# A reduction over three numbers for the softmax sums, and another order of work, in a fused attention, expert and gated-convolution kernel

## The chip, the cores and the metric

One core of a Trainium2 chip runs one program. The metric is the device time of one execution in microseconds (us), as the median of several runs. Five engines work side by side: TensorE (PE, matmuls), VectorE (DVE), ScalarE (ACT), GpSimd (POOL), and SyncE (SP), which here only issues DMAs.

## What is computed

Three layers on a batch of 4 with 576 positions, in float32. Cut to what matters:

```
# 1. attention, 8 heads of 64, twice per head: on q, k, v averaged by 4, and in a band of |i-j| < 4
out_up    = repeat(softmax(q_d @ k_d.T / 8) @ v_d, 4)
out_local = softmax(where(band, q @ k.T / 8, -1e9)) @ v
x = (out_up + out_local) laid out as (4, 576, 512)
# 2. four experts with causal attention, each position takes its best two
for e in range(4):
    s = where(causal, -1e9, (x @ wq[e]) @ (x @ wk[e]).T / 8);  s -= s.max(-1)
    a = exp(s);  a /= a.sum(-1) + 1e-09
    out += gate(e) * (a @ (x @ wv[e]) @ wo[e])
# 3. gated convolution with 5 taps
gate = 1 / (1 + exp(-conv(out)))
y = (gate * (out @ w_val)) @ w_out
```

## The kernel before

Nearly every product is done in three matmuls: both operands are split into a high and a low part in a faster 32-bit type, and high x high, low x high and high x low are summed in PSUM (`mm3`, its matmuls at L1228, L1229 and L1230). The split is a cast (L798) and a subtraction (L815), on an engine of choice. The weights w_val, w_o and w_out come in a 64-bit type; `chunk` (L817) loads their raw words and makes float32 of them: two absolute values on ACT (L854, L859), two steps on DVE (L863, L867), an addition on POOL (L871) and a merge on DVE (L875). `weights_tail` (L889) multiplies w_o by w_val (L896) once, so that layer 2 ends in w_o x w_val. `weights_qkv` loads and splits the experts' weights wqk and wvg.

The attention goes through four batches and four pairs of heads. For each pair the q and k rows are averaged (L946, L953, giving qd and kd), the averaged scores are made on PE (L1083), their maximum is taken on DVE (L1007) and scaled by the scale factor (L1017, on ACT or POOL), the exponentials are made on ACT, either with the sum (L1022) or without (L1028, the sum then on DVE at L1042 or L1044), normalized (L1070 or on ACT at L1068), transposed on PE (L1099) and copied out of PSUM (L1106, pdT). L1117 multiplies by v. The band's part does the same in blocks of 64 rows: scores at L1142 and L1148, transposes at L1161, copies at L1168 (pT), values at L1183; L1200 adds the two parts into a row, which is then split into xh and xl for the experts.

The experts go over two pairs of experts (pr) and five tiles T of 128 queries (the last has 64). `expert_scores` makes the scores (L1380), `exponentials` masks them and finds the extremes (L1410) and makes the exponentials with their sums on ACT (L1419). `weigh` (L1468) adds EPS to the sums, takes the reciprocal (L1491) and multiplies the exponentials by it and the gate's weight (L1520, or on ACT at L1517). For the last tile, two experts lie one under the other on the partitions and the sum comes in two pieces, one per half of the keys, in a buffer of the pool `es`. `keys_on_rows` transposes the weighted exponentials (L1441, into two PSUM banks) and copies them out (the helper `copy`, L790, buffer mp), and L1552 multiplies them by the values (vE). The gated convolution follows: taps at L1600 to L1619, the product with w_out, and a copy (L1646) and store (L1652) of the result.

The order of all this isn't the order of the code. Each step is a `piece` with an engine, a cost in us, and the buffers it reads and writes. `Plan.order` (L358) goes through a model of the five engines; where an engine is free it takes, of the pieces whose inputs and buffers are there, the one with the earliest entry in the table `DUE` (L34), one entry for each of 2773 pieces in the order of their creation. Where a step can go to several engines, `pick` (L311) takes the option whose number stands in the string `PICK` (L255), 1008 characters. The instructions are then issued in the order found, and each engine works through its own in that order. The numbers of the buffers and PSUM banks (ps_63 to ps_70) follow from it.

```
p = Piece(engine, cost, late, (DUE[idx] if idx < len(DUE) else 0.0, idx), fn, k, size)
...
k = min(int(PICK[n]), len(options) - 1) if n < len(PICK) else 0
```

Of the kernel before, what the change touches and what calls it, by code (L numbers as in the profile page):

```python
# [21 lines left out]
EPS = 1e-9  # L22
# [12 lines left out]
    0.3, 1.5, 0.7, 5.45, 1.6, 0, 0.15, 3.85, 3.6, 5.2, 4.58, 0.5, 6.19, 2, 3.88, 4.83, 0, 1, 9.28, 4.5,  # L35
    16.58, 3.52, 4.1, 6.05, 6.81, 0.5, 1.5, 6, 22.88, 5, 4.59, 5.08, 6.73, 7.22, 17.54, 18.54, 7.78,
    10.77, 11.82, 12.71, 12.29, 12.29, 14.5, 15.06, 15.35, 10.26, 11.2, 11.67, 11.89, 12.93, 14.04,
    14.63, 14.92, 16.62, 18.95, 18.53, 21.15, 22.48, 24.1, 12.93, 15.14, 15.84, 16.3, 16.3, 15.74,
    15.74, 16.3, 18.4, 19.77, 19.98, 15.54, 16.14, 16.14, 16.14, 16.3, 18.17, 19.37, 20.11, 20.98,
    21.27, 22.24, 23.25, 23.67, 24.3, 25.31, 25.72, 29.93, 30.84, 26.62, 27.82, 28.67, 29.8, 19.93,  # L40
    21.38, 22.41, 22.86, 22.88, 21.98, 21.98, 22.88, 24.96, 26.51, 26.86, 21.77, 22.37, 24.74, 22.81,
    22.37, 22.37, 22.81, 26.84, 27.4, 27.62, 28.69, 30.31, 30.41, 31.47, 32.48, 32.71, 33.81, 34.55,
    32.6, 35.41, 36.28, 37.2, 14.58, 16.08, 25.52, 29.42, 29.92, 19, 19.57, 22.52, 23.1, 21.38, 21.88,
    26.02, 33.48, 32.48, 26.15, 28.09, 27.07, 28.76, 38.08, 39.1, 25.08, 26.61, 27.49, 28.05, 27.82,
    27.2, 27.2, 27.82, 30.15, 32.11, 32.82, 27, 29.09, 30.66, 29.47, 27.6, 27.6, 29.47, 33.14, 33.4,
    33.62, 30.15, 31.59, 32.53, 33, 32.99, 34.03, 35.12, 36.22, 36.51, 32.2, 33.65, 34.31, 34.31, 35.7,
    36.42, 37.11, 37.42, 39.01, 40.64, 40.64, 43.37, 45.19, 45.36, 41.49, 42.74, 43.77, 44.96, 46.38,
    46.38, 47.01, 47.83, 46.38, 46.81, 47.39, 47.9, 34.03, 36.31, 37.91, 38.37, 38.41, 36.91, 36.91,
    39.9, 40.54, 41.15, 41.44, 36.71, 38.34, 38.81, 42.74, 37.31, 37.31, 44.12, 44.72, 45.59, 45.88,
    47.39, 48.66, 49.08, 49.87, 50.88, 51.19, 52.95, 53.68, 50.88, 50.88, 51.49, 51.88, 8.78, 16.41,  # L50
    16.83, 2.5, 7.96, 8.58, 4, 14.11, 14.72, 2, 7.58, 8.04, 23.38, 32.18, 34.17, 3, 8.93, 9.66, 22.38,
    29.18, 30, 15.08, 19.59, 20.38, 0, 6.42, 6.65, 6.88, 6.19, 5.5, 3.5, 10.65, 11.27, 11.42, 11.89,
    12.43, 13.81, 14.7, 18.02, 17.08, 15.58, 21.3, 21.85, 22.17, 22.9, 23.64, 25.02, 27.4, 25.97, 35.97,
    26.52, 39.99, 39.44, 41.24, 41.71, 42.79, 44.52, 50.65, 48.22, 62.46, 68.35, 72.56, 73.44, 73.47,
    74.01, 74.55, 75.98, 76.87, 79.31, 78.06, 0, 79.68, 80.5, 0, 81.49, 25.02, 31.29, 36.67, 28.92,
    38.23, 39.56, 91.07, 95.14, 95.28, 95.87, 96.51, 97.05, 98.35, 98.89, 98.73, 103.73, 104.59, 104.68,
    105.49, 106.54, 108.62, 110.24, 111.36, 45.41, 54.53, 55.08, 55.3, 56.23, 56.77, 58.25, 59.13,
    59.78, 59.13, 63.3, 63.85, 64.07, 64.78, 65.52, 67.02, 70.22, 70.96, 76.87, 81.7, 82.25, 82.63,
    84.21, 85.88, 87.59, 90.08, 91.52, 65.82, 66.18, 66.54, 66.9, 68.83, 68.15, 61.71, 62.07, 63.23,
    65.46, 66.35, 67.23, 57.48, 57.84, 58.2, 58.56, 60.29, 61.81, 53.46, 53.82, 54.54, 55.79, 56.81,  # L60
    60.56, 31.01, 38.28, 49.42, 54.18, 56.96, 54.82, 69.17, 69.57, 68.61, 69.91, 71.18, 71.73, 69.39,
    69.77, 72.45, 73.28, 73.82, 74.35, 74.87, 75.46, 80.78, 86.85, 69.38, 72.38, 72.73, 73.09, 73.99,
    74.54, 67.77, 68.23, 68.58, 69.73, 70.76, 70.32, 71.4, 73.44, 73.8, 74.15, 74.51, 75.65, 77.73,
    62.43, 63.59, 63.95, 65, 65.69, 65.69, 66.69, 35.55, 40.41, 52.92, 55.34, 59.18, 59.75, 58.94,
    59.51, 56.57, 57.15, 68.94, 70.09, 70.53, 71.83, 73.12, 72.61, 75.06, 54.9, 56.15, 56.59, 57.03,
    59.74, 62.55, 60.61, 62.88, 60.01, 62.31, 60.28, 60.83, 61.27, 62.79, 64.72, 64.4, 66.76, 7.44,
    7.33, 75.07, 76.67, 77.37, 76.94, 77.71, 78.06, 78.66, 78.55, 79.15, 79.82, 80.28, 80.55, 81.28,
    80.55, 81.83, 80.55, 81.43, 80.55, 82.35, 84.81, 86.38, 86.94, 89.84, 91.58, 92.29, 94.55, 95.43,
    99.19, 81.02, 82.36, 82.87, 82.09, 83.22, 83.81, 86.47, 85.07, 87.06, 87.75, 88.6, 88.88, 89.98,
    89.28, 90.6, 88.88, 90.96, 88.88, 89.22, 92.83, 94, 93.62, 94.92, 96.19, 96.19, 96.85, 97.13, 98,  # L70
    87.32, 88.67, 91, 89.38, 91.73, 94.37, 95, 95.27, 96.2, 95.27, 97.18, 98.5, 99.23, 99.31, 91.95,
    93.13, 94.48, 93.87, 95.52, 97.22, 99.77, 100.05, 103.44, 100.05, 101.53, 106.64, 109.82, 107.8,
    93.33, 96.78, 95.07, 98.53, 99.11, 99.6, 101.15, 104.61, 105.42, 105.83, 106.13, 107.27, 108.59,
    110.76, 113.29, 117.58, 117.19, 118.22, 111.81, 114.29, 116.07, 113.17, 116.63, 117.9, 119.75,
    120.02, 120.76, 120.02, 120.12, 125.38, 127.44, 126.58, 116.85, 117.91, 119.34, 118.65, 120, 121.41,
    121.93, 122.23, 124.79, 122.13, 124.17, 128.2, 129.16, 128.95, 118.11, 122.42, 119.38, 123.13,
    123.62, 126.11, 126.96, 127.71, 128.18, 128.46, 128.46, 129.82, 130.39, 131.42, 133.4, 135.96,
    135.96, 136.76, 32.98, 33.98, 40.59, 54.73, 61.46, 42.03, 43.17, 45.21, 45.72, 34.97, 35.47, 40.09,
    60.96, 61.96, 46.71, 47.61, 49.91, 50.48, 51.61, 52.74, 46.15, 48.26, 48.85, 49.2, 49.2, 48.85,
    48.85, 49.2, 51.29, 52.61, 53.33, 49.51, 50.11, 51.07, 50.56, 50.11, 50.11, 50.56, 53.19, 54.92,  # L80
    58.55, 51.61, 54.04, 54.69, 57.22, 55.02, 55.02, 60.22, 61.1, 62.84, 53.53, 54.56, 55.63, 54.89,
    54.89, 61.19, 61.72, 62.28, 64.3, 65.23, 65.84, 75.86, 77.3, 77.51, 67.26, 69.88, 70.2, 77.83,
    78.83, 78.95, 80.31, 82.86, 78.83, 79.38, 79.93, 80.8, 58.92, 60.08, 60.68, 60.68, 60.68, 61.32,
    61.92, 63.12, 65.04, 65.75, 66.04, 61.91, 63.2, 68, 63.67, 62.51, 62.51, 63.67, 70.62, 71.09, 72.2,
    80.27, 81.01, 81.35, 81.92, 82.93, 83.38, 84.3, 85, 82.93, 83.08, 83.92, 87.12, 48.12, 47.62, 54.23,
    78.83, 79.33, 57.39, 60.48, 55.04, 56.01, 59.96, 60.46, 53.73, 82.93, 90.57, 64.41, 64.98, 68.25,
    68.81, 61.02, 77, 70.97, 72.77, 75.58, 76.04, 76.05, 76.05, 77.97, 78.46, 79.24, 72.25, 73.03,
    74.25, 73.37, 73.37, 75.85, 77.2, 78.17, 83.58, 84.55, 85.47, 86.19, 88.31, 91.56, 78.61, 80.75,
    82.8, 83.27, 83.56, 81.35, 81.35, 85.98, 86.92, 87.41, 87.7, 80.35, 81.15, 84.59, 81.48, 80.95,
    80.95, 81.48, 86.99, 87.5, 88.89, 91.08, 92.56, 92.71, 93.95, 95.15, 95.44, 96.46, 97.23, 95.15,  # L90
    96.2, 96.84, 98.35, 88.42, 90.56, 91.16, 91.16, 91.16, 91.91, 92.9, 94.6, 96.85, 97.51, 97.8, 91.18,
    91.78, 91.78, 91.78, 92.31, 93.26, 97.6, 99.11, 99.84, 100.7, 102.31, 103.05, 103.39, 104.34,
    105.35, 105.93, 106.8, 107.4, 105.45, 105.91, 107.78, 110.42, 97.26, 99.82, 100.44, 100.41, 101.05,
    100.41, 101.84, 100.41, 102.63, 100.41, 103.82, 105.14, 103.63, 103.98, 106.69, 107.49, 108.42,
# [1618 lines left out]
```

## Time and profile before

| | |
|---|---|
| median of 3 runs | 355.61 us (353.96 to 356.92) |
| profiled execution | 357.07 us, its span 355.4 us |
| PE busy | 332.9 us (94%) |
| DVE busy | 297.4 us (84%) |
| ACT busy | 257.8 us (73%) |
| POOL busy | 204.7 us (58%) |
| mean granted TensorE clock | 0.974 |

The span runs from the first to the last recorded instruction; 1.7 us of the execution lie around it. Busy times are shares of the whole span, so a view by windows is needed to see in which stage an engine is short of work. In the rows, L12 is line 12 of the kernel before; "A <- B" behind an idle time names the instruction whose end let A start. The granted clock is 1.00 at 2.4 GHz and 0.50 at 1.2 GHz.

### The profile page before, as it was taken

The numbers are of one execution on the slowest core, as the hardware profiler recorded it, in microseconds if no ns is written. First come the engines' busy times: TensorE is split into PE (matmuls) and PEld (weight loads), VectorE is DVE, ScalarE is ACT, GpSimd is POOL, SyncE is SP. The second block draws the span as 40 slices with busy tenths as digits, with TensorE's granted clock in tenths as the row PEclk, the third lists the DMA queues.
The fourth block names the chain that finished last, engine by engine and source line by source line (L and its number), as shares of the span: only waits on it lengthen the run. The fifth ranks groups of instructions, "written<-read, shape, count | busy, mean of one in ns | idle before, by whom it ended". The sixth has DMA issues, their size and how long they took to land.

```text
span 355.4 us, 11539 instructions
## 1 busy us (share of the span) xinstructions
PE 332.9 (94%) x4360; PEld 290.8 (82%) x4360; DVE 297.4 (84%) x921; ACT 257.8 (73%) x923; POOL 204.7 (58%) x325
## 2 busy tenths in 40 slices
PE   0697899998999999999999999999999999999996
PEld 0464679876698898999898897998998899997896
DVE  6898998899999899988989786898887668799572
ACT  3778968689888987688786797466765565688462
POOL 7357867559879852477978432384673036444070
PEclk9999589997899999999999999999999999999999
DMA  7979948519431344236222110101000100001022
GB/s 264 258 217 236 235 137 184 155 61 195 110 85 50 91 123 113 52 107 169 65 91 68 50 51 2 39 4 70 9 0 5 44 0 17 0 4 57 15 65 74
DMA packets 26279, 31.70 MB, mean 89 GB/s; under 512 B 2672, under 2 KB 18032, under 8 KB 26224
## 3 DMA queue, kind: packets, MB, share of 16 engines
q1 hardware_dynamic: 26224, 30.97, 32.4%
q8 instruction: 34, 0.56, 0.7%
q14 instruction: 21, 0.17, 0.2%
HBM read 26.24 MB, written 4.72 MB: 87 GB/s over the span
## 4 chain that ended last, share of the span: by engine, by line
PE 81%; DVE 9%; POOL 4%; ACT 3%; issue 2%; POOLq 0%; DVEq 0%
PE ps L1228 19%; PE ps L1229 17%; PE ps L1230 17%; PE ps L1552 7%; PE ps L1380 5%; PE ps L1441 3%; PE ps L1183 2%; PE ps L1148 2%; PE ps L896 2%; PE ps L1117 1%; PE ps L1161 1%; PE ps L1083 1%; DVE mx L1007 1%; ACT p L1022 1%; PE ps L1099 1%
## 5 line engine op out<-in xcount | busy, mean ns | idle before, releaser
L1419 ACT ACTIVATE pe<-ps,mmin 128x128 f32<-128x128 f32 (+4 forms) x80 | 41.9, 527 | 15.3 <-DVE mmin L1410 10.0
L1612 POOL TENSOR_TENSOR row<-row,row 128x256 f32<-128x256 f32 (+1 forms) x40 | 32.0, 804 | 33.0 <-ACT row L1607 18.4
L1614 DVE SCALAR_TENSOR_TENSOR row<-ps,cw,row 128x320 f32<-128x320 f32 (+1 forms) x88 | 43.3, 513 | 6.2 <-ACT row L1600 4.3
L1228 PE MATMUL ps<-gh,wout_h 128*128 128x256 f32 (+1 forms) x128 | 39.3, 307 | 0.5 <-DVE pT L1168 0.5
L1230 PE MATMUL ps<-xh,wqk_l 128*128 128x256 f32 (+1 forms) x128 | 37.8, 295 | 2.1 <-POOL wqk_l L815 2.1
L1228 PE MATMUL ps<-xh,wqk_h 128*128 128x256 f32 (+1 forms) x128 | 39.1, 306 | 0.6 <-DVE vE L790 0.3
L1229 PE MATMUL ps<-gl,wout_h 128*128 128x256 f32 (+1 forms) x128 | 37.8, 295 | 0.0
L1229 PE MATMUL ps<-xl,wqk_h 128*128 128x256 f32 (+1 forms) x128 | 37.8, 295 | 0.0
L1230 PE MATMUL ps<-gh,wout_l 128*128 128x256 f32 (+1 forms) x128 | 37.7, 294 | 0.0
L1552 PE MATMUL ps<-mp,vE 128*64 128x320 f32 (+4 forms) x224 | 27.0, 374 | 0.0
L1230 PEld LDWEIGHTS ps<-xh,wqk_l 128*128 128x128 f32 x128 | 24.2, 189 | 2.3 <-POOL wqk_l L815 2.3
L1228 PEld LDWEIGHTS ps<-gh,wout_h 128*128 128x128 f32 x128 | 24.1, 188 | 2.5 <-POOL gl L815 0.8
L1228 PEld LDWEIGHTS ps<-xh,wqk_h 128*128 128x128 f32 x128 | 24.1, 189 | 2.2 <-DVE vE L790 0.6
L1520 POOL TENSOR_SCALAR pe<-pe,rs,gw 128x128 f32<-128x128 f32 (+3 forms) x31 | 21.0, 683 | 7.8 <-DVE mmin L1415 4.9
L1007 DVE TENSOR_REDUCE mx<-ps 128x5 f32<-128x320 f32 (+1 forms) x48 | 23.7, 519 | 1.1 <-PE ps L1148 0.6
L1229 PEld LDWEIGHTS ps<-gl,wout_h 128*128 128x128 f32 x128 | 24.1, 188 | 0.2 <-POOL gl L815 0.2
L1229 PEld LDWEIGHTS ps<-xl,wqk_h 128*128 128x128 f32 x128 | 24.2, 189 | 0.0
L1230 PEld LDWEIGHTS ps<-gh,wout_l 128*128 128x128 f32 x128 | 24.1, 188 | 0.0
L1228 PE MATMUL ps<-wvg_h,xh 128*128 128x260 f32 (+1 forms) x80 | 23.5, 293 | 0.6 <-POOL xh L798 0.6
L1552 PEld LDWEIGHTS ps<-mp,vE 128*64 128x64 f32 (+1 forms) x224 | 14.2, 138 | 11.9 <-issue 3.9
L1230 PE MATMUL ps<-wvg_h,xl 128*128 128x260 f32 (+1 forms) x80 | 22.7, 284 | 1.0 <-DVE xl L815 1.0
L1229 PE MATMUL ps<-wvg_l,xh 128*128 128x260 f32 (+1 forms) x80 | 22.6, 282 | 0.0
(231 smaller groups left out, 1208.8 us busy)
## 6 DMA issues: line engine op xcount, KB each, us to landing
qt<-in_qT_dram SPq DMA_DIRECT2D x16, 288.0 KB, 3.7
kt<-in_kT_dram SPq DMA_DIRECT2D x16, 288.0 KB, 4.4
v<-in_vx_dram SPq DMA_DIRECT2D x16, 288.0 KB, 5.3
vw<-in_vx_dram SPq DMA_DIRECT2D x16, 192.0 KB, 4.1
out_dram<-o SPq DMA_DIRECT2D x16, 160.0 KB, 1.8
raw<-in_w_val_dram SPq DMA_DIRECT2D x4, 512.0 KB, 5.1
vw<-in_vx_dram SPq DMA_DIRECT2D x16, 128.0 KB, 3.9
raw<-in_w_out_dram SPq DMA_DIRECT2D x4, 512.0 KB, 3.5
```

Source lines behind the costliest of these rows:

```text
L896: nc.tensor.matmul(pw[m].t, t.t[:, m * P:(m + 1) * P], f.t, start=(c == 0), stop=(c == KC - 1))
L1007: nc.vector.tensor_reduce(out=mx.t[:n, :g, 1], in_=sv(), op=ALU.max, axis=AX.X)
L1228: nc.tensor.matmul(p, ah, bh, start=first, stop=False)
L1229: nc.tensor.matmul(p, ah, bl, start=False, stop=False)
L1230: nc.tensor.matmul(p, al, bh, start=False, stop=last)
L1380: nc.tensor.matmul(s.t[:, o:o + P * (t + 1)], a.t[r, P * t:P * t + P], z.t[r, :P * (t + 1)], start=(k == 0 and t == T[0]), stop=(k == 2 an ...
L1419: nc.scalar.activation(pe.t[:, off + c0:off + c1], s.t[:, o:o + c1 - c0], AF.Exp, bias=m.t[:, 0:1], scale=-1.0, accum_out=sums.t[:, a:a + ...
L1441: nc.tensor.transpose(pt.t[:, i:i + 64], pe.t[r, j * P:(j + 1) * P], ident[r, r])
L1520: ENG[en].tensor_scalar(v, v, x, y, op0=ALU.mult, op1=ALU.mult)
L1552: nc.tensor.matmul(av.t[64 * e:64 * e + 64, z:n], vE.t[:kr, j, 2 * pr + e, :], pT.t[:kr, e, k0:k0 + n - z], start=(j == 0), stop=(j == Tl))
L1612: nc.gpsimd.tensor_add(g.t[:, :nn], g.t[:, :nn], g2.t[:, :nn])
L1614: nc.vector.scalar_tensor_tensor(g.t[:, :nn], x2.t[:, k:k + nn], cw.t[:, m, k:k + 1], g.t[:, :nn], op0=ALU.mult, op1=ALU.add)
```

## The change

Four edits are in the code, and both tables are new. The buffers of `es` get four columns; the third of them holds EPS from the start on, and for the last tile of a pair the two pieces of the sum and EPS are added by one reduction over three columns into the fourth, of which the reciprocal is taken. This happens eight times, once for each batch and pair. Of the 2773 due times 2754 are other numbers, and 443 of the 1008 choices of an engine (or of the order of two things) are others.

```diff
 DUE = (
-    0.3, 1.5, 0.7, 5.45, 1.6, 0, 0.15, 3.85, 3.6, 5.2, 4.58, 0.5, 6.19, 2, 3.88, 4.83, 0, 1, 9.28, 4.5,
+    0.3, 1.8, 0.7, 5.35, 0, 0.5, 0.65, 1.6, 5.95, 6.65, 1.85, 0.8, 6.19, 0, 1.9, 4.15, 0, 1, 6.5, 4.5,
...
 PICK = (
-    "011100000001230000010112021100012002032101000120010100100011231130040010001000000150042211001021"
+    "010100000032210001001202021100012012030100000100000100000031231142040001010101100152040201021021"
...
-        "es": slots("es", 2, [P, 2]),
+        "es": slots("es", 2, [P, 4]),
...
             nc.vector.memset(t[:, :, 1], EPS)
+        for t in pools["es"]:
+            nc.vector.memset(t[:, 2:3], EPS)
...
-                nc.vector.tensor_scalar(sums.t[:, 0:1], sums.t[:, 0:1], sums.t[:, 1:2], EPS, op0=ALU.add, op1=ALU.add)
+                nc.vector.tensor_reduce(out=sums.t[:, 3:4], in_=sums.t[:, 0:3], op=ALU.add, axis=AX.X)
...
-            nc.vector.reciprocal(a, a)
+            nc.vector.reciprocal(a, sums.t[:, 3:4] if last else a)
```

Lines of the changed kernel lie 1 to 3 below those of the kernel before: L857 is L854, L862 is L859, L1020 is L1017, L1444 is L1441. Over the whole program DVE has 905 instructions in place of 923, ACT 775 in place of 747, POOL 333 in place of 330; PE's matmuls and SP's 137 DMAs stay as many.

First place: ACT in the first 15 us, around the first piece of w_val (raw_80 holds its words, o_164 and o_165 the two operands; mx_84 and mx_85 are the maxima of the first averaged scores). Before:

```order
L1527 ACTIVATE ah_157<-ident 128x2x4
L854 ACTIVATE o_164<-raw_80 128x512
L1017 ACTIVATE mx_84<-mx_84 128x3
L859 ACTIVATE o_165<-raw_80,two 128x512
L1017 ACTIVATE mx_85<-mx_85 128x3
L1028 ACTIVATE pd_95<-ps_64,mx_84 128x3x48 x3
L1022 ACTIVATE pd_95,sm_88<-ps_63,mx_85 128x3x48 x3
```

Now:

```order
L1530 ACTIVATE ah_157<-ident 128x2x4
L801 CAST wvg_h<-o_164 128x260
L1020 ACTIVATE mx_84<-mx_84 128x3
L857 ACTIVATE o_164<-raw_80 128x512
L862 ACTIVATE o_165<-raw_80,two 128x512
L1025 ACTIVATE pd_95,sm_88<-ps_64,mx_85 128x3x48 x3
L1031 ACTIVATE pd_95<-ps_63,mx_84 128x3x48 x3
```

The scaling of mx_84 stands ahead of both absolute values (L857, L862), where it stood between them (L854, L859); a split of wvg stands ahead of all, and the scaling of mx_85 is now a reduction on DVE (L1018, L1015 before).

Second place: POOL around the last piece of wqk (o_164 is its load, o_166 is w_o's, p_93 a block of band exponentials). Before:

```order
L815 TENSOR_TENSOR wqk_l<-o_165,wqk_h 128x512
L798 CAST wo_h<-o_166 128x512
L798 CAST wqk_h<-o_164 128x512
L1070 TENSOR_TENSOR p_93<-p_93,sm_90 128x320
L1017 TENSOR_SCALAR mx_85<-mx_85 128x3
L815 TENSOR_TENSOR wqk_l<-o_164,wqk_h 128x512
L1200 TENSOR_TENSOR row_103<-row_103,od_101 128x228
```

Now:

```order
L801 CAST wqk_h<-o_164 128x512
L818 TENSOR_TENSOR wqk_l<-o_163,wqk_h 128x512
L801 CAST wo_h<-o_166 128x512
L1020 TENSOR_SCALAR mx_84<-mx_84 128x3
L1020 TENSOR_SCALAR mx_85<-mx_85 128x3
L1073 TENSOR_TENSOR p_93<-p_93,sm_90 128x320
L818 TENSOR_TENSOR wqk_l<-o_164,wqk_h 128x512
L1203 TENSOR_TENSOR row_106<-row_106,od_101 128x228
```

The cast of the last piece (wqk_h from o_164) has moved ahead of the wait for w_o; its lo part (wqk_l from o_164) still stands behind the cast of w_o, two scalings and the normalization p_93.

Third place: ACT around the second pair's first exponentials of the experts, some 80 us into the run (pe_135 and pe_136 are the exponentials, L1419 or L1422; p_92 and p_93 are blocks of the band's). Before:

```order
L854 ACTIVATE o_164<-raw_80 128x512
L859 ACTIVATE o_165<-raw_80,two 128x512
L1017 ACTIVATE mx_85<-mx_85 128x5
L1419 ACTIVATE pe_135,rs_145<-ps_66,mmin_137 128x128
L1419 ACTIVATE pe_136,rs_145<-ps_67,mmin_141 128x128
L1028 ACTIVATE p_92<-ps_69,mx_85 128x64 x5
L1022 ACTIVATE p_93,sm_89<-ps_65,mx_84 128x64 x5
```

Now:

```order
L862 ACTIVATE o_163<-raw_80,two 128x512
L1020 ACTIVATE mx_85<-mx_85 128x5
L857 ACTIVATE o_164<-raw_80 128x512
L1031 ACTIVATE p_92<-ps_70,mx_85 128x64 x5
L1025 ACTIVATE p_93,sm_88<-ps_63,mx_84 128x64 x5
L1109 COPY pdT_96<-ps_69 112x432
L1422 ACTIVATE pe_135,rs_145<-ps_64,mmin_141 128x128
L1422 ACTIVATE pe_136,rs_145<-ps_65,mmin_137 128x128
L801 CAST wout_h<-o_163 128x512
```

The band's exponentials (L1031, L1025) stand ahead of the experts' (L1422), and a copy of pdT has come to ACT.

On PE, at the same place, the transposes L1441 came right behind the 18 transposes L1099; in the changed kernel the values L1186 (40 small matmuls, L1183 before) stand between them, and the band's scores (L1145 and L1151) stand ahead of L1120 (L1117 before).

## Rows read from the trace of the kernel before

**Rows 1.** The page, parts 1 and 2: busy time by engine; busy tenths of PE by slice.

```profile
PE 332.9 (94%) x4360; PEld 290.8 (82%) x4360; DVE 297.4 (84%) x921; ACT 257.8 (73%) x923; POOL 204.7 (58%) x325
...
PE   0697899998999999999999999999999999999996
...
PEclk9999589997899999999999999999999999999999
```

**Rows 2.** Three windows: us, then busy us (instructions) of PE, PEld, DVE, ACT, POOL; clock; DMA.

```profile
0.00:100.00 100.00, 81.22 (x1270) 63.24 (x1271) 89.33 (x272) 77.05 (x320) 70.80 (x119) 0.91 0.72 184
100.00:350.00 250.00, 249.47 (x3079) 225.66 (x3079) 207.59 (x650) 179.42 (x601) 133.94 (x207) 1.00 0.18 50
350.00:355.40 5.40, 2.19 (x15) 1.93 (x14) 0.49 (x1) 1.31 (x3) 0.00 (x0) 0.90 0.34 121
```

**Rows 3.** PE's waits: line waited for, us in total, times, longest.

```profile
PE ps L1083 <- POOL kd L953: 8.1, 1, 8.1
PE ps L896 <- DVE o L875: 3.2, 1, 3.2
PE ps L1230 <- POOL wqk_l L815: 2.1, 1, 2.1
PE ps L1230 <- DVE xl L815: 1.0, 1, 1.0
PE ps L1441 <- ACT p L1028: 0.7, 1, 0.7
...
PE ps L1441 <- DVE p L1033: 0.7, 1, 0.7
```

**Rows 4.** Windows around the stalls and the low clock, columns as in rows 2.

```profile
34.00:38.00 4.00, 0.88 (x3) 0.38 (x3) 2.92 (x8) 3.13 (x12) 3.93 (x6) 0.86 1.16 230
36.00:48.00 12.00, 10.32 (x159) 8.14 (x159) 11.40 (x23) 8.80 (x32) 9.52 (x12) 0.57 0.85 217
50.00:100.00 50.00, 47.65 (x685) 39.37 (x685) 46.05 (x155) 42.68 (x176) 38.28 (x52) 0.93 0.54 132
84.00:92.00 8.00, 7.27 (x107) 5.48 (x107) 7.55 (x24) 7.95 (x37) 7.67 (x11) 0.57 0.71 126
```

**Rows 5.** PE's timeline: start, us, form, count; in brackets idle before and releaser.

```profile
14.47 2.08 PE L896 MATMUL ps<-o,row 128*128 128x512 f32 x2 [3.20 <-DVE o L875]
...
25.77 1.98 PE L896 MATMUL ps<-o,row 128*128 128x512 f32 x4
```

**Rows 6.** DVE's groups by form: count, busy us, mean ns, idle before and releaser.

```profile
L790 DVE COPY mp<-ps 128x384 f32<-128x384 f32 x15 | 8.0, 551 | 2.1 <-PE ps L1441 2.1
...
L1168 DVE COPY pT<-ps 128x348 f32<-128x348 f32 x15 | 7.4, 508 | 0.3 <-PE ps L1161 0.3
...
L1106 DVE COPY pdT<-ps 112x432 f32<-112x432 f32 x10 | 5.9, 596 | 0.0
...
L790 DVE COPY vE<-ps 128x256 f32<-128x256 f32 x9 | 3.8, 417 | 0.1
...
L1477 DVE TENSOR_SCALAR es<-es 128x1 f32<-128x1 f32 x8 | 1.7, 209 | 1.4 <-ACT pe L1419 1.4
...
L1053 DVE TENSOR_REDUCE sm<-sm 128x5 f32<-128x10 f32 x7 | 1.1, 155 | 0.0
```

**Rows 7.** Timelines of ACT and POOL at the first piece of w_val.

```profile
10.02 0.68 ACT L854 ACTIVATE o<-raw 128x512 f32<-128x512 f32 x1 [1.91 <-DMA raw<-in_w_val_dram]
11.00 0.21 ACT L1017 ACTIVATE mx<-mx 128x3 f32<-128x3 f32 x1 [0.30 <-DVE mx L1007]
...
12.43 1.26 POOL L871 TENSOR_TENSOR o<-o,o 128x512 int32<-128x512 int32 x1 [3.99 <-DVE o L867]
```

**Rows 8.** POOL's timeline around the last piece of wqk.

```profile
31.69 0.61 POOL L798 CAST wo_h<-o 128x512 fp32r<-128x512 f32 x1 [1.40 <-DMA o<-in_wo_dram]
...
34.23 1.26 POOL L815 TENSOR_TENSOR wqk_l<-o,wqk_h 128x512 fp32r<-128x512 f32 x1
```

**Rows 9.** PE's timeline at 82 us.

```profile
81.81 0.91 PE L1183 MATMUL ps<-pT,vw 64*64 64x58 f32 x40
```

More of the change, by code (lines that the diff above doesn't have):

```diff
@@ L34 @@
 DUE = (
[217 rows of a table removed]
[218 rows of a table added]
 )
 PICK = (
-    "011100000001230000010112021100012002032101000120010100100011231130040010001000000150042211001021"
-    "212000102110110000002121012101010100110000111000010000010000001111000000000100111111120211000001"
-    "001011102000101100222011001010001001003203201021101111010210012000120002102100100101110222121110"
-    "400100010010012202220000012000000100000110110110000000100000000001000011200000010000100011111000"
-    "100111001110010100101010010010101012110112122001002000101101201012011112010001011110110111322002"
-    "100132251111101121202220000010010111111010421420222020000000001121212221000110011001210001210111"
-    "110000200000010020000021000021000021101000101100010001110000110010010110011011001001210101111021"
-    "101011220000110011111211012211001010100101010120222130210011011100110140052211001011110100111152"
-    "130201102011010000012132101101011110001021110010101100010010001111110100002101110001000000110110"
-    "110100011101010010111011000010100000011022112010011100010022101001002110002000120100010000001110"
-    "110010002110010011010000210000211111200100000010"
+    "010100000032210001001202021100012012030100000100000100000031231142040001010101100152040201021021"
+    "010111002110112000002101210110010000010111010001001100000010001010000011000100111111110011000001"
+    "000210001000021100212101011010111101000010014200220100000210212204120002102100000001112000021000"
+    "420010000010012202120000002100102100000000100100110100100000010001000001211100200000101110100010"
+    "011000001100110101110010111101102111100002021000002111101200100012000110000010100111111111022322"
+    "010141150201101120202322001010111101000111202400020221000100001110210221111010210000201000201100"
+    "011000210010001001010001000020010000010111110100100010111010101010110110100000010111200110110022"
+    "201000201102001000110211112010020000100011101000240130042001001001100030041210000001111111101142"
+    "240042141101100012010141050110111120100120000111010021011101010101102001112011000100002000011001"
+    "000110111001111111100011111100100000110022002110111001001010100110101001102201110100011000110010"
+    "000000000100102101100100210010211100010100000110"
 )
```

433 rows, old and new, of the table DUE are left out of this document.

## Prediction

> **What bounds the kernel now.** I read the page first: PE is busy for 332.9 of 355.4 us, DVE for 297.4, and in the 40 slices of the span PE falls short of nine tenths mainly in the first quarter and in the last slice [rows 1]. The chain of waits that ended last runs through PE for most of its length, so the views that matter are those that say where PE stands idle and where its clock is low. Three long windows give the first [rows 2]: in the first 100 us PE is busy for 81.22, so idle for 18.8; from 100 to 350 us it is idle for 0.53 of 250; behind 350 us it is idle for 3.2 while the last output is copied and written. An order of work can only win what stands in those 22.5 us, and what a low clock costs. The products are the same: both orders hold equally many matmuls of each form.
>
> PE's waits name the idle time [rows 3]. Its first matmul comes at 8.07 us, when POOL has made the first down-sampled k. It waits 3.2 us for the first piece of w_val made from its 64-bit words, 2.1 and 1.0 us for two lo parts between 34 and 38 us, and 0.7 us twice at L1441. These last two belong to the 2.35 us that PE is idle between 50 and 100 us [rows 4].
>
> The windows from 36 to 48 and from 84 to 92 us have a mean granted clock of 0.57 [rows 4]: the full level (2.4 GHz) gives way to the half (1.2 GHz) and comes back. Taken as all work, 12 x 0.43 = 5.2 us and 8 x 0.43 = 3.4 us of full clock are missing. Ahead of the first fall PE had been busy for 0.88 of 4 us (34 to 38); the second came at about the first wait at L1441, of 0.7 us. At the start the clock row shows nine tenths or more [rows 1], but I go by the durations: a pair of L896 took 2.08 us at 14.47 and four took 1.98 at 25.77 [rows 5], so the first 20 us went at half pace too.
>
> **The four edits of code.** Eight times the sum of two accumulators and a constant goes from a tensor_scalar with its second operand as a scalar per partition (209 ns each) to a tensor_reduce over three numbers of one tile. The nearest row is the reduction of ten numbers to five at L1053, 155 ns [rows 6]. So 8 x 0.05 = 0.4 us leaves DVE; two memsets of one column each come in at the start. All eight places lie behind 100 us, where PE is idle for 0.53 us in all and DVE has 42 us to spare [rows 2]. I take 0; bounds -0.4 and +0.1 (the memsets, if they hold up the first add).
>
> **The order and the engines.** DVE issues 18 instructions fewer, ACT 28 more, POOL 3 more. The largest moves: 12 copies of L790 (8 mp, 4 vE), 5 of L1168 and 3 of L1106 go from DVE to ACT, at 0.55, 0.42, 0.51 and 0.60 us [rows 6]: 4.4 + 1.7 + 2.5 + 1.8 = 10.4 us. Against it casts of qh and normalizations come to DVE, so that some 6 of its 297 us go. In the body that buys nothing, since PE waits for nobody there; what counts is the first 100 us, place by place.
>
> *Start, 0 to 20 us.* POOL's add of the k rows goes to DVE and the loads alternate q and k, so the first of two kd tiles is ready earlier; but PE's first group needs the second kd too, and that stands behind one more add on DVE. No gain taken. For w_val, ACT's scaling of mx now stands ahead of the absolute value that starts the conversion. In the trace the absolute value starts at 10.02 and the scaling only at 11.00, when DVE's maximum is there [rows 7]. So the conversion starts 1.0 us later. Its other operand and POOL's step at 12.43 [rows 7] were waiting for DVE and ACT in any case, so I count half as left: the product starts near 14.95 in place of 14.47. Both its halves then run back to back, where 18 transposes stood between them, and PE has 0.5 us less behind it at 20 us; but it then waits for ACT again, so the loss is mostly covered. I take 0; bounds -0.7 (kd's early half) and +0.8.
>
> *28 to 40 us.* The stall of 2.1 us is the lo part of the last piece of wqk. On POOL it stood behind a wait of 1.40 us for wo from DMA, two casts, a normalization and a scaling, and started at 34.23 for 1.26 us [rows 8]. In the new order the cast of that piece is moved ahead, but the lo part of another piece, the cast of wo with its DMA, two scalings and the same normalization still stand before it. On SP's queue that piece is still the last load of wqk, behind the same bytes. By the same durations it ends between 35.1 and 35.8. I take 0; bounds -1.5 (the wait for wo gone) and +0.5.
>
> *80 to 95 us.* Before, L1441 came right behind the transposes L1099, and PE waited 0.7 us for ACT, which had two w_val steps and two exponentials of L1419 ahead of the one that freed the bank. Now the 0.91 us of L1183 [rows 9] stand between L1099 and L1441 and cover that wait, and ACT has the band's exponentials ahead of those of L1419 (the two w_val steps stay ahead). The second wait has L1441 pulled ahead of the next scores, which may cover it or lay it bare. Of the 2.35 us I take about half as gone, 1.1 us, for this and the lighter DVE together; bounds -2.35 (all) and +1.0 (L1441 bare).
>
> *Body and tail.* 0.1 us of the stall of about 0.5 in the body; bounds -0.5 and +1.5, the upper end being two new stalls of L1441's kind. Between the last w_o product and the first group of the last chunk equally many matmuls stand in both orders, and behind the last matmul come the same copy and stores: 0, within 0.3.
>
> **Sum.** 0 + 0 + 0 - 1.1 - 0.1 = -1.2 us. The profiled execution took 357.07 us (its span of 355.4 and 1.7 around it), so it would take 355.9. It lies 1.46 above the median of the runs, 355.61; the forecast for the median is 354.4. All bounds on one side give -5.8 and +4.2, without the clock.
>
> **Rivals.**
> *A fall of the clock does not come.* Each fall follows thin work. L1183 behind L1099 and the band's scores ahead of L1117 fill the stretch before the second; an earlier lo part of wqk would fill the one before the first. Against it: the stalls at 34 to 38 us stay by my count. Without the second fall 354.4 - 3.4 = 351.0 us; without the first 349.2; without both 345.8.
>
> *The start holds the clock down (the slower side).* Place: the wait for the w_val product, now some 3.7 us long. Price: if the full level comes later by as much work as the fall at 36 us held, 5.2 us, 354.4 + 5.2 = 359.6 us. It decides once the four L896 at 25 us take 4 us in place of 1.98. For it: the pace doubled only after that wait, and the first fall followed a stretch with as little work. Against it: DVE holds the pace until 30 us, so part of the price is hidden, and both halves of the product back to back are denser work than before.
> The Trainium skill (TensorE: Matmul & The Clock Gate, section "HAM oscillation — how this bites in real kernels") says that an engine left waiting between bursts of matmuls is put back to the low clock and runs the start of the next burst at it. The trace agrees at 36 us (0.57). At 14.47 us it cannot tell, since the pace was low already. By the page alone this rival would be the likelier one.
>
> *Nothing takes effect.* The stalls move and add up to the same, and the gain in DVE lies in covered work: 355.6 us.
>
> **How the numbers follow.** One per cent, 3.6 us, is about what a measurement of this kernel tells from no change: faster means under 352.05, slower over 359.2. The forecast, with its own range of 352 to 357, gets 0.48; nothing takes effect 0.15; one fall gone 0.20 and both 0.04; the start holds the clock down 0.13. Nearly all of the falls gone is faster, 0.24, and the forecast's own tail adds 0.06. Of the slow start half stays under 359.2 because part hides behind DVE, so 0.07, and new stalls and the forecast's other tail add 0.06. So faster 0.30, same 0.57, slower 0.13. The range leaves out both falls gone and the end of the slow cases: 348.5 to 358.8.
>
> **What would show it.** Right: PE idle in the first 100 us between 16.5 and 19; the w_val product's first matmul near 14.95; a wait of about 2 us at the lo part of wqk; both dips of the clock still there; at most 0.4 us of wait at the first L1441; 0.6 us or less idle from 100 to 350 us; the new reductions at 140 to 160 ns. Wrong: a wait at L1441 of 1 us; four L896 at 25 us in 4 us; a clock of 1.00 throughout 84 to 92 us; a body idle for over 2 us; or a gain in the body while PE was busy there, which would mean that the matmuls' own durations depend on the order.

## The result, and the profile after

The changed kernel took 359.39 us (median of 4 runs, 357.96 to 360.34) beside 354.78 us for the kernel before on the same chip: 1.0118 of its time, 95% interval 1.0077 to 1.0159. It is slower by about 4.6 us, where 1.2 us less had been forecast, and it lies 0.6 us above the range. A second series gave 361.12 beside 355.11 us, 1.0159 (1.0135 to 1.0183). Two executions of later versions, of 405.33 us (the edits alone, mean clock 0.757) and 363.08 us (the tables alone), count as slow ones: they are in the medians below, not in the ratios, which are taken over the other runs and so are not exactly quotients of two medians.

The profiled execution of before that the prediction read took 357.07 us, more than any other run of its series. For the comparison I use a second profiled execution of the same kernel, of 355.07 us and a span of 353.4, which is nearer to the median.

The page of the changed kernel, parts 1 and 2 (profiled execution 358.89 us, span 357.2):

```profile
PE 334.5 (94%) x4360; PEld 290.5 (81%) x4360; DVE 291.5 (82%) x903; ACT 262.1 (73%) x929; POOL 206.5 (58%) x328
...
PE   1686999996999999999999999999999999999996
...
PEclk9999589999699999999999999999999999999999
```

DVE lost the 6 us that were forecast (291.5 in place of 297.4, [rows 1]) and ACT gained 4. PE has grown: 334.5 us, against 332.9 in [rows 1] and 330.4 in the second profile.

The changed kernel in the windows of [rows 2], the last to its end:

```profile
0.00:100.00 100.00, 80.62 (x1263) 61.63 (x1264) 84.70 (x261) 78.73 (x318) 72.73 (x121) 0.91 0.68 182
100.00:350.00 250.00, 249.86 (x3073) 225.15 (x3072) 205.32 (x641) 182.34 (x610) 133.76 (x207) 1.00 0.19 51
350.00:357.20 7.20, 3.99 (x28) 3.73 (x26) 1.48 (x3) 1.02 (x3) 0.00 (x0) 1.00 0.26 92
```

And the second profile of the kernel before, in the same windows:

```profile
0.00:100.00 100.00, 80.72 (x1285) 63.48 (x1286) 89.72 (x279) 78.90 (x326) 73.62 (x122) 0.90 0.74 189
100.00:350.00 250.00, 249.47 (x3077) 225.57 (x3075) 205.91 (x644) 178.00 (x597) 132.07 (x204) 1.00 0.17 49
350.00:353.40 3.40, 0.18 (x2) 0.00 (x0) 0.00 (x0) 0.44 (x1) 0.00 (x0) 0.92 0.36 128
```

PE's idle time is 22.7 us after (357.2 less 334.5) and 23.0 before (353.4 less 330.4). So PE does not wait longer. It is busy 4.1 us longer with the same matmuls, and a list of waits can't show such a loss.

PE's waits after, for [rows 3]:

```profile
PE ps L1086 <- POOL kd L956: 6.7, 1, 6.7
PE ps L899 <- DVE o L878: 3.5, 1, 3.5
PE ps L1164 <- ACT p L1071: 1.6, 2, 1.4
PE ps L1102 <- ACT pd L1071: 1.5, 1, 1.5
PE ps L1444 <- ACT p L1031: 0.8, 1, 0.8
...
PE ps L1233 <- POOL wqk_l L818: 0.8, 1, 0.8
...
PE ps L1383 <- ACT pe L1422: 0.5, 2, 0.3
```

The start is 1.4 us earlier, the lo part of wqk is waited for 0.8 us in place of 2.1, and the body waits for 0.14 us in place of 0.53. In exchange there are waits for ACT that were not there: 1.5 at L1102, 1.4 and 0.2 at L1164, 0.5 at L1383. The wait for ACT at L1444 is the old one at L1441, with 0.8 us in place of 0.7.

Where the time went is seen in three windows. The columns are those of [rows 2]; the last but two is the granted clock. After:

```profile
36.00:48.00 12.00, 11.40 (x160) 8.34 (x161) 8.29 (x19) 7.60 (x27) 9.84 (x12) 0.57 0.72 180
80.00:90.00 10.00, 7.19 (x170) 5.22 (x167) 9.74 (x36) 9.73 (x43) 8.95 (x14) 1.00 0.77 193
90.00:100.00 10.00, 9.49 (x93) 7.00 (x92) 8.15 (x25) 7.99 (x27) 7.93 (x11) 0.66 0.08 25
```

The kernel before, second profile:

```profile
36.00:48.00 12.00, 10.96 (x175) 8.57 (x179) 11.39 (x23) 8.25 (x33) 8.54 (x11) 0.60 0.95 236
80.00:90.00 10.00, 8.96 (x160) 6.70 (x157) 9.54 (x33) 9.91 (x45) 9.67 (x15) 0.66 0.61 139
90.00:100.00 10.00, 9.55 (x129) 8.14 (x126) 9.93 (x36) 8.60 (x31) 8.44 (x13) 1.00 0.51 153
```

The first fall, of 36 to 48 us, is in both. The second has moved. Before, it lies in 80 to 90 us (0.66), and from 90 to 100 us PE has the full clock, with DVE busy for 9.93 us of 10. After, 80 to 90 us has the full clock and 90 to 100 has 0.66. There PE is busy for 9.49 us, while DVE and ACT have fallen to 8.15 and 7.99: their longest waits there are for PE (ACT 1.6 us for L1444, DVE 1.3 us for L1186). PE's timeline of the changed kernel around it:

```profile
82.52 0.58 PE L1444 MATMUL ps<-ident,pe 64*128 64x64 f32 x11 [0.81 <-ACT p L1031]
...
88.64 0.28 PE L1164 MATMUL ps<-ident,p 64*128 64x64 f32 x2 [1.43 <-ACT p L1071]
...
90.68 0.50 PE L1383 MATMUL ps<-kh,qh 64*128 64x512 f32 x1 [0.28 <-ACT pe L1422]
...
92.01 1.05 PE L1383 MATMUL ps<-kh,ql 64*128 64x512 f32 x2
...
94.01 1.54 PE L1186 MATMUL ps<-pT,vw 64*64 64x58 f32 x40
...
96.31 1.55 PE L1555 MATMUL ps<-mp,vE 128*64 128x256 f32 x8
```

The wait of 1.43 us that ends at 88.64 is followed by shorter ones of 0.20 and 0.28 us, and from 91.1 to 97.9 us the clock is at its half level (1.2 GHz). The forty matmuls of L1183, now L1186, take 1.54 us there and took 0.91 at the full level [rows 9].

To put a number on it I took for every group of matmuls of one line and shape the lower quartile of its time at the full clock over the profiles, and added up what PE had done by a given time (in us of such work, 283.8 in all):

| profile | done by 90 us | done by 100 us | lost in 90 to 100 | last matmul ends | lost from 100 to there |
|---|---|---|---|---|---|
| before, second | 46.5 | 54.4 | 2.1 | 350.2 | 20.8 |
| before's tables with the edits | 46.9 | 54.5 | 2.4 | 350.2 | 20.9 |
| after, first | 46.8 | 51.6 | 5.2 | 354.0 | 21.8 |
| after, second | 46.6 | 51.0 | 5.6 | 354.6 | 21.8 |
| the new tables without the edits | 46.3 | 50.4 | 6.0 | 355.3 | 21.9 |

At 90 us the two orders stand level. In the next ten us the new order loses 3.1 to 3.9 us more than the second profile of before, some 3.4 in the mean, and 1.0 us in the 250 behind them. The low stretch of 6.8 us at half the clock is 3.4 us of full clock.

### The profile page after: what moved, and what is told of

Its sections match the earlier page's. It is cut to its first block, busy times and chain, and to the rows that moved or that the text cites. A ratio compares the mean times of both kernels' runs of the same rounds, so it can differ in the third digit from the quotient of the medians.

```text
span 357.2 us, 11534 instructions
## 1 busy us (share of the span) xinstructions
PE 334.5 (94%) x4360; PEld 290.5 (81%) x4360; DVE 291.5 (82%) x903; ACT 262.1 (73%) x929; POOL 206.5 (58%) x328
## 4 chain that ended last, share of the span: by engine, by line
PE 82%; DVE 6%; POOL 4%; ACT 3%; DMA 2%; issue 1%; SPq 1%; POOLq 0%; ACTq 0%; DVEq 0%
PE ps L1231 19%; PE ps L1232 17%; PE ps L1233 17%; PE ps L1555 7%; PE ps L1383 5%; PE ps L1444 3%; PE ps L1186 3%; PE ps L1164 2%; DMA raw<-in_w_val_dram 2%; PE ps L1151 2%; PE ps L1120 2%; PE ps L1086 2%; PE ps L899 1%; DVE mx L1010 1%; POOL row L1615 1%
## 5 line engine op out<-in xcount | busy, mean ns | idle before, releaser
L1422 ACT ACTIVATE pe<-ps,mmin 128x128 f32<-128x128 f32 (+4 forms) x80 | 41.8, 528 | 13.2 <-DVE mmin L1413 10.3
L1615 POOL TENSOR_TENSOR row<-row,row 128x256 f32<-128x256 f32 (+1 forms) x38 | 30.7, 811 | 34.5 <-DVE row L1617 19.8
L1617 DVE SCALAR_TENSOR_TENSOR row<-ps,cw,row 128x320 f32<-128x320 f32 (+1 forms) x90 | 44.4, 512 | 7.6 <-ACT row L1610 3.1
L1231 PE MATMUL ps<-xh,wqk_h 128*128 128x320 f32 (+1 forms) x128 | 39.1, 305 | 0.1
L1233 PE MATMUL ps<-xh,wqk_l 128*128 128x320 f32 (+1 forms) x128 | 37.9, 296 | 0.8 <-POOL wqk_l L818 0.8
L1232 PE MATMUL ps<-xl,wqk_h 128*128 128x320 f32 (+1 forms) x128 | 37.8, 295 | 0.0
L793 ACT COPY mp<-ps 128x384 f32<-128x384 f32 (+2 forms) x43 | 19.9, 504 | 9.7 <-PE ps L1444 5.4
L1523 POOL TENSOR_SCALAR pe<-pe,rs,gw 128x384 f32<-128x384 f32 (+3 forms) x29 | 18.8, 651 | 12.2 <-DVE rs L1494 6.9
L1232 PE MATMUL ps<-wvg_l,xh 128*128 128x260 f32 (+1 forms) x80 | 22.7, 284 | 0.0
```

Source lines behind the costliest of these rows:

```text
L793: (nc.scalar.copy if eng == "act" else ENG[eng].tensor_copy)(out(), src())
L1231: nc.tensor.matmul(p, ah, bh, start=first, stop=False)
L1232: nc.tensor.matmul(p, ah, bl, start=False, stop=False)
L1233: nc.tensor.matmul(p, al, bh, start=False, stop=last)
L1422: nc.scalar.activation(pe.t[:, off + c0:off + c1], s.t[:, o:o + c1 - c0], AF.Exp, bias=m.t[:, 0:1], scale=-1.0, accum_out=sums.t[:, a:a + ...
L1523: ENG[en].tensor_scalar(v, v, x, y, op0=ALU.mult, op1=ALU.mult)
```

## The experiments

Theory A, and A1 in its sharper form: the new order loses its time where the second fall of the clock lies. A fall costs nothing where ACT and DVE hold the pace, and nearly all of its missing clock, half its length, where PE does. Rivals: the new reduction (B), chance in the clock from run to run (C), the body (A2), and ACT and DVE holding the pace at 90 us as well (A3). All ratios are to runs of the kernel before on the same chip.

**Both kernels once more.** No edit.

> The kernel before, unchanged, once more. Theory A (the new order of work loses time, mostly where PE waits for ACT between 80 and 92 us): ratio 1.00, with PE idle 1.1 to 1.7 us between 80 and 92 us. Theory B (the reduction in weigh costs the time): ratio 1.00. Theory C (the difference of 4.6 us is a matter of how often the clock of TensorE falls in one run or another, and the two orders are alike): runs spread over 353 to 360 us with mean clocks from 0.960 to 0.977.

354.86 us, ratio 0.9988 (0.9969 to 1.0008). In its profile PE waits for 1.4 us between 80 and 92 us.

> The changed kernel, unchanged, once more. Theory A: 1.010 to 1.014 of the kernel before, with the same waits for ACT between 80 and 92 us in the new trace (3.2 us in all). Theory B: the same ratio. Theory C: a ratio within 0.5% of 1, and runs of both kernels that take the same time where their clocks are the same.

361.12 us, 1.0159, with the same waits for ACT between 80 and 92 us as in the first profile (1.6, 0.8 and 0.5 us) and the low clock at 92.4 to 99.2. Theory C falls: runs of before with mean clocks of 0.965 and of 0.981 lie within 2 us of each other, and the slowest of them (357.67) is faster than the fastest of after in this series (359.49).

**The edits alone, and the tables alone.** The edits with the numbers of before, and the reverse:

```diff
 DUE = (
-    0.3, 1.8, 0.7, 5.35, 0, 0.5, 0.65, 1.6, 5.95, 6.65, 1.85, 0.8, 6.19, 0, 1.9, 4.15, 0, 1, 6.5, 4.5,
+    0.3, 1.5, 0.7, 5.45, 1.6, 0, 0.15, 3.85, 3.6, 5.2, 4.58, 0.5, 6.19, 2, 3.88, 4.83, 0, 1, 9.28, 4.5,
...
```

> The four edits of code (reduction over three columns) with the two tables of the kernel before: the order of work is that of before. Theory A: ratio 0.998 to 1.002, the reduction at 140 to 170 ns in place of 209. Theory B: ratio 1.008 to 1.015. Theory C: within 0.5% of 1.

355.33 us, 1.0003 (0.9985 to 1.0021). The reduction in that kernel (min, median and max in ns):

```profile
L1479 DVE TENSOR_REDUCE es<-es x8: 138/150/157, 103.0 to 328.5; 128x1 f32<-128x3 f32 x8
```

It takes 150 ns in place of the 209 of [rows 6], and it is worth nothing, as forecast.

> The kernel before with the two new tables and none of the four edits: the order of work is that of the changed kernel. Theory A: ratio 1.010 to 1.014, as the changed kernel. Theory B: 1.000 to 1.003. Theory C: within 0.5% of 1.

359.25 us, 1.0100 (1.0060 to 1.0140). Theory B falls: within the intervals the whole loss is in the two tables. Of its six runs one took 355.31 us, as the kernel before. The order alone does not fix the time, then. What made that execution fast isn't known: it was not profiled, and its mean clock, 0.976, is that of two slower ones (358.63 and 359.87 us).

**The order up to 95 us of one kernel, from there of the other.** Each due time and each choice is taken from one table or the other by the time at which the first kernel's order starts the piece:

```diff
-DUE = the changed table
+DUE[i] = before[i] if begin[i] < 95 else changed[i]
```

> Before's due times and engines for all pieces that before's order starts by about 95 us, the changed ones for the rest (on PE the first 731 instructions are before's, the last 2250 of 3142 the changed kernel's). Theory A1 (nearly all of the loss of 4 to 5 us is in 90 to 100 us, where the low clock of 6.8 us now falls on dense matmuls while in the kernel before it fell on a stretch in which PE waits for ACT and DVE in any case): 355 to 356.3 us, ratio 1.000 to 1.004, low clock at 83 to 91 us. Rival A2 (the body from 100 us on is slower, by stalls too short for the list of waits): 358 to 359.5, ratio 1.009 to 1.013.

360.27 us, 1.0155. Outside what either theory gave. The low clock lay at 84.4 to 87.8 us, about where A1 had put it, and yet the kernel was slow. Its trace has new waits behind the seam, of which the two longest are:

```profile
PE ps L1231 <- DVE row L1617: 1.4, 1, 1.4
PE ps L1444 <- DVE p L1036: 1.2, 1, 1.2
```

> The changed due times and engines for all pieces that the changed order starts by about 95 us, before's for the rest (on PE the first 743 instructions are the changed kernel's, the last 2195 of 3142 before's). Theory A1: 358 to 360 us, ratio 1.008 to 1.014, low clock at 91 to 98 us. Rival A2: 355 to 356.5, ratio 1.000 to 1.004.

360.90 us, 1.0169, above what A1 gave, with the low clock at 91.3 to 98.1 us as A1 had it. Its seam has one wait:

```profile
PE ps L1232 <- DVE xl L818: 1.4, 1, 1.4
```

Work done by 100 us was 53.1 in the first, between before (54.4) and after (51.6), and 50.9 in the second, as after. But PE is idle for 4.3 us between 90 and 150 us in the first, where the second profile of before has 0.45, and for 1.4 us at the seam in the second. So the two times decide nothing between A1 and A2: this order, cut and joined, brings waits of its own. What stands against A2 is the table above, with 1.0 us lost behind 100 us of some 4.4.

**The wait filled.** Six matmuls of the identity by itself, ahead of the transposes that wait at 88.64 us, into the bank that these overwrite:

```diff
         def _():
+            if key == "12":
+                for _ in range(6):
+                    nc.tensor.matmul(pts[0].t[:, :P], ident, ident, start=True, stop=True)
             for h, p in enumerate(ps):
```

> The changed kernel with six added matmuls of the identity by itself (128x128, f32) on PE ahead of the transposes L1164 of the seventh head pair, into the bank that these overwrite; they can run in the wait of 1.4 us for ACT at 88 us, and nothing else moves. Theory A1: with that wait filled the clock does not fall at 91 us, the granted clock is 1.00 from 90 to 100 us, and the kernel gets faster with more work: 355.5 to 357.5 us, ratio 1.001 to 1.007. Rival A3 (the fall is a consequence of something else, or the pace there is set by ACT and DVE): 359 to 361, ratio 1.010 to 1.017, low clock of 6.8 us at 91 us as before.

355.72 us, 1.0022 (1.0002 to 1.0041). With more work the kernel is 3.7 to 5.4 us faster than the changed kernel's two medians. Windows of its trace, then the added matmuls (12 on the engine) and the transposes behind them:

```profile
80.00:90.00 10.00, 9.07 (x172) 7.13 (x171) 9.70 (x33) 9.87 (x44) 8.38 (x13) 0.83 0.88 197
90.00:100.00 10.00, 9.77 (x132) 8.24 (x131) 9.55 (x34) 9.76 (x36) 9.66 (x16) 1.00 0.22 68
```

```profile
89.09 1.60 PE L1162 MATMUL ps<-ident 128*128 128x128 f32 x12
90.62 0.58 PE L1167 MATMUL ps<-ident,p 64*128 64x64 f32 x12
```

From 90 to 100 us the clock is 1.00, and DVE and ACT are up at 9.55 and 9.76 us. The clock still fell, but at 85.2 us and for 3.4 us, in the stretch where ACT and DVE hold the pace. Rival A3 falls: all twelve runs (354.59 to 357.60 us) are faster than all nine of the changed kernel (357.96 to 361.29).

How the filling does this is not seen in the profiled execution. Its fall began 3.9 us ahead of the first added matmul, so these can't have moved it there, and PE came to them without a wait, because it had run the work ahead of them at half the clock. What can be put down to the filling is less low clock over the runs: the mean clock is 0.979 to 0.990 in eleven of the twelve, and 0.960 to 0.976 in the nine of the changed kernel (a rough measure, since the low clock of the start is recorded in some executions only).

**The same six matmuls in the body** (`key == "32"`), as the control.

> Control for the run with the filled wait: the same six added matmuls at the transposes of the fifteenth head pair, some 230 us into the run, where PE is always busy. Every theory: the changed kernel plus 0.6 to 1.4 us, 360 to 361.5 us, ratio 1.012 to 1.018; low clock at 91 to 98 us unchanged.

359.89 us, 1.0159 (1.0113 to 1.0205), six runs from 358.40 to 363.60. The low clock of the profile lay at 88.7 to 95.5 us, 2.4 us ahead of what was expected, and still on the matmuls behind the wait. So it was not the matmuls as such that helped, but their place.

**Two in place of six** (`range(2)`).

> The changed kernel with two in place of six added matmuls in the wait at 88 us, some 0.4 of its 1.4 us. Theory A1 (the idle time of PE ahead of 91 us decides when the clock falls, and how much dense work it then hits): between the two, 356 to 359 us, ratio 1.004 to 1.012, where the low clock begins before 90 us or lasts 3.4 us in the profile if the time is at the fast end, and 6.8 us from 91 us if it is at the slow end. Rival A4 (the six matmuls helped by something else, such as the bank being written earlier): the same as with six, 355.7 us.

358.79 us, 1.0123 (1.0087 to 1.0159). A third of the filling leaves nearly the whole loss: 0.78 us of the wait remained, and the fall stays behind 90 us. Rival A4 falls.

```profile
80.00:90.00 10.00, 7.85 (x169) 5.58 (x165) 9.76 (x35) 9.86 (x43) 9.62 (x14) 1.00 0.81 184
90.00:100.00 10.00, 9.59 (x89) 7.24 (x90) 8.13 (x30) 7.99 (x29) 7.74 (x13) 0.66 0.09 27
```

**The wait ahead of the first fall filled, in the kernel before.** Matmuls by zeros that are added to the open sum:

```diff
         nc.tensor.matmul(p, ah, bl, start=False, stop=False)
+        if fill:
+            idle(fill[0], p, fill[1], zer[:, :fill[2]], bh, False)
```

> The kernel before with added matmuls by a tile of zeros that add nothing to the open sums: twelve in the wait of 2.1 us for the lo part of wqk at 34 us, seven in the wait of 1.0 us for xl at 36 us. Theory A1 (low clock costs where dense work of PE follows and nothing else holds the pace): the first fall, of 10.2 us at 36 us, gets shorter or goes; but DVE is busy for 11.4 of the 12 us behind it, so of the 5 us only 0 to 2.5 come back: 352.5 to 355 us, ratio 0.993 to 1.000. Rival A5 (PE's pace decides there too): 350 to 351.5 us, ratio 0.986 to 0.990.

355.88 us, 1.0024 (1.0006 to 1.0043): no gain at all, 0.9 us past the slow end of what A1 gave. Its trace shows the added matmuls and the window behind them:

```profile
32.76 1.92 PE L660 MATMUL ps<-xh,zer 128*128 128x320 f32 x12
...
35.43 0.98 PE L660 MATMUL ps<-wvg_h,zer 128*64 128x260 f32 x7
```

```profile
36.00:48.00 12.00, 9.89 (x188) 7.37 (x189) 11.37 (x24) 8.14 (x34) 8.48 (x11) 0.86 0.91 236
```

The low stretch shrank from 10.2 to 3.4 us and the clock of the window rose from 0.60 to 0.86. DVE is busy for 11.37 of the 12 us, as before. So the 6.8 us of low clock that went away had cost nothing, with DVE busy nearly throughout. Rival A5 falls, and with it the 5.2 us at which the prediction had priced this fall.

**Three waits filled, in the changed kernel.** The six at 88 us, five by zeros at the lo part of wqk, six ahead of the second L1102.

> The changed kernel with the wait at 88 us filled by six matmuls, and also five by a tile of zeros in the wait for the lo part of wqk at 34 us and six of the identity in the wait for ACT ahead of the transposes L1102 at 35 us. Theory A1: the changed kernel with one wait filled (355.7) less 0 to 2.5 us: 353 to 355.7 us, ratio 0.995 to 1.002. Rival A5: 350.5 to 352.5, ratio 0.987 to 0.993.

356.31 us, 1.0069 (1.0042 to 1.0097), over A1's upper end. Its twelve runs lie in two groups: eight from 355.69 to 357.19 us and four from 359.01 to 359.82. The profiled one is of the second group, and its fall lies at 92.5 to 99.4 us. In that execution the wait at 88 us had shrunk to 0.17 us, and the clock fell all the same: filling this wait made times of 359 us and more rarer but does not rule the fall out, and what else sets it is open. The mean clocks go with the groups, 0.984 to 0.989 in seven of the eight and 0.971 to 0.981 in the four; that the first group has no fall on dense work is argued from this, since only one run is profiled. The first fall shrank from 10.2 to 6.8 us (41.4 to 48.2) and gave nothing back here either, though DVE is busy for only 8.29 of 12 us in this window of the changed kernel: in its place PE waited 1.2 us for ACT at 39.6 us.

**Less work for ACT and DVE at 80 to 90 us.** The conversion of the last piece of w_out gets later due times (its load 97 in the changed kernel, 100 in the kernel before; its eight steps by 20 and 24):

```diff
-DUE[350], DUE[351:359] = 77.2, d
+DUE[350], DUE[351:359] = 97, d + 20
```

> The changed kernel with later due times for the conversion of the last piece of w_out (two ACT and three DVE steps, the POOL steps and the cast: from 81 to 89 us to 101 to 109, its load behind that of the taps). Theory A1 with its cause A6 (PE waits between 80 and 91 us because ACT and DVE have more work there than fits, some 1.7 us of it this conversion): less than 1.5 us of waits for ACT from 80 to 92 us in place of 3.2, the low clock begins before 88 us or lasts 3.4 us, 354 to 357 us, ratio 0.998 to 1.006. Rival A7 (the waits come from the order of the softmax steps and stay): waits of 3 us and the low clock at 91 us stay, 358 to 361 us, ratio 1.009 to 1.017.

360.45 us, 1.0155 (1.0125 to 1.0184). The waits from 80 to 92 us:

```profile
PE ps L1164 <- ACT p L1071: 1.4, 1, 1.4
PE ps L1383 <- DVE mp L793: 0.6, 1, 0.6
```

They went from 3.2 to 2.0 us, of which 1.4 for ACT, so the load of ACT and DVE is part of them (A6). But the longest, 1.4 us at L1164, stayed (A7), and the low clock lay at 87.9 to 98.2 us, longer and on dense work again. What A1 with A6 had asked for (under 1.5 us of waits for ACT, a fall that begins before 88 us) came about, and its time did not: where a fall begins does not say how long it lasts. By the sum of work used above the run stood some 0.6 us ahead of the changed kernel at 100 us; it lost more behind, where PE is idle for 1.6 us between 100 and 150 us and in the changed kernel never.

> The kernel before with the same later due times for the conversion of the last piece of w_out. Theory A1 with A6: ACT and DVE hold the pace from 80 to 91 us, so 0.5 to 1.7 us come back: 353 to 354.5 us, ratio 0.995 to 0.999. Rival A7: no gain, or a loss by the pieces that move with it: 354.8 to 357 us, ratio 1.000 to 1.006.

362.06 us, 1.0205 (1.0166 to 1.0243). Neither theory gave that. Windows:

```profile
80.00:90.00 10.00, 8.31 (x190) 6.48 (x188) 9.70 (x37) 9.50 (x46) 8.46 (x15) 1.00 0.98 213
90.00:100.00 10.00, 10.00 (x127) 8.80 (x125) 9.47 (x34) 9.03 (x33) 9.29 (x16) 1.00 0.36 102
100.00:350.00 250.00, 246.44 (x3008) 219.14 (x3008) 207.74 (x635) 176.41 (x593) 129.66 (x199) 1.00 0.17 50
```

There is no second fall any more and 90 to 100 us is full at 1.00, but the pieces that moved with it leave PE idle for 3.56 us of the 250 us behind, where [rows 2] had 0.53. By the sum of work used above it stood 1.6 us ahead of the second profile of before at 100 us, as A1 with A6 had it, and lost 8.7 us on it in the stretch behind. The idle time is 3.0 of these. The rest went while PE counts as busy at the full clock, and its cause was not found: a body can lose several us that no wait and no clock shows. No version here beats the kernel before.

## Why the prediction was wrong

*Start.* The product of w_val began at 14.55 us, not 14.95, and its four matmuls ran back to back:

```profile
14.55 3.78 PE L899 MATMUL ps<-o,row 128*128 128x512 f32 x4 [3.47 <-DVE o L878]
...
24.75 1.98 PE L899 MATMUL ps<-o,row 128*128 128x512 f32 x4
```

Four of the same took 1.98 us at 24.75, as in [rows 5]. So the slower rival, the start holding the clock down, did not come about. The term of 0 held, the level of work by 90 us being the same, but partly by luck: PE's first wait was 1.4 us shorter (6.7 in place of 8.1), which the prediction had not taken and whose bound was 0.7, and later waits took it back.

*28 to 40 us.* The lo part of wqk was waited for 0.8 us, not 2; ACT's pd took its place with 1.5 us. The sum of 0 held.

*80 to 95 us.* This is the term that failed, -1.1 in the sum. It counted waits alone: L1441 covered by L1183, and 1.1 of 2.35 us gone. The cover did not work: at L1444 the wait was 0.8 us, where at most 0.4 was to show the forecast right and 1 us to show it wrong, and the next transposes got 1.6 us that no step had foreseen, because ACT's normalization (L1071) came behind four exponentials, a copy and the cast of w_out. PE was idle for 19.4 us of the first 100, where 16.5 to 19 had been forecast. Even so the waits did not cost the time: by 90 us the orders stand level. What cost it was the clock. The prediction left the second fall out of its sum as something that stays, and as a rival priced it at its missing clock, 3.4 us, wherever it lay. In fact it had cost before next to nothing, as it lay under a stretch in which ACT and DVE hold the pace (with a low stretch of 3.4 in place of 6.8 us, the kernel with the edits alone had done as much by 100 us, 54.5 and 54.4). Moved by some 7 us, onto matmuls that nothing else delays, it cost about its full price: 3.4 us. The sign that was to show a fall gone, full clock throughout 84 to 92 us, nearly came (it fell at 91.1), and meant a fall moved.

*The rivals' prices.* By the same mistake the first fall was worth 5.2 us in the list of rivals; measured, in the kernel before, two thirds of it going (6.8 of 10.2 us) was worth nothing. That a longer wait would leave the clock low where it hurts was the mechanism of the slower rival, at the wrong place and with a chance of 0.13. The Trainium skill (TensorE: Matmul & The Clock Gate, section "HAM oscillation — how this bites in real kernels") says that an engine left waiting between bursts runs the next burst at the low clock. This trace agrees in kind at 91 us: 0.66 in 90 to 100 us behind waits of 1.43, 0.20 and 0.28 us, which are for ACT, where the page's case waits for DMA.

*Body.* Forecast as -0.1, measured as a loss of 1.0 us with 0.4 us less of waiting. The three profiles of the new order agree within 0.1. Which matmuls lose it is not shown: they overlap, and the answer changes with the way in which shared time is given to one or the other. The cause was not tried.

*The edits.* As forecast: 140 to 157 ns, no effect on the time.

Open: why the clock fell at 84 us before and at 91 after, beyond that the longest of PE's waits there ends at 88.6 us in place of 84.7 and is twice as long (with that wait filled it still fell at 92.5 in one profile); what the body loses while PE counts as busy; and whether an order exists that has no fall at 80 to 100 us without waits behind it.

## What to carry to other kernels

A fall of TensorE's clock is not a fixed cost: read in the same window which engine is full. Here a half-speed PE was free where DVE or ACT had 9.5 of 10 us, and was paid for in full where they dropped to 8 and PE stayed at 9.5. This is a reading to be tested, by filling the wait ahead of the fall, and not a rule: with DVE at 8.29 of 12 us a shorter fall gave nothing back either, since ACT held PE up next. When two orders wait equally long and one has more busy time on PE, compare the clock window by window before looking for a stall. And a wait can be worth filling with useless matmuls, if dense work follows it: six of them gave back most of 4.6 us, though with two more waits filled a third of the runs stayed slow.

## What was not expected of the hardware

A kernel got faster by added work: 359.39 to 355.72 us with six matmuls that compute nothing. The low stretches after the start lasted between 3.4 and 13.7 us. In the profile of the changed kernel the granted clock is shown as 1.00 for the first 20 us, while a group of four matmuls took 3.78 us at 14.55 and 1.98 us at 24.75; the second profile of the same kernel has 0.85 there. So at the start the durations have to be read in place of the column.
